# Softmax sums of batches 2 to 7: VectorE copies and additions in place of four TensorE products per batch

## The chip, the cores and the metric

The kernel runs on one core of a Trainium2 chip. The metric is the device time of one execution in microseconds (us). TensorE is called PE in the profile (its weight loads PEld), VectorE is DVE, ScalarE is ACT, GpSimd is POOL, and SyncE, which only issues DMAs here, is SP.

## The reference

Grouped-query attention (8 batches, 16 query heads on 4 key heads, 384 positions, head size 64) feeds a mixture of experts with a gate in two levels (4 groups of 4 experts; 3072 tokens of width 1024).

```python
scores = scale * np.matmul(q, k.transpose(0, 1, 3, 2))      # k, v repeated for each group of heads
scores = scores - np.max(scores, axis=-1, keepdims=True)
attn = np.exp(scores)
attn = attn / (np.sum(attn, axis=-1, keepdims=True) + 1e-09)
x = np.matmul(attn, v)                                       # then (B, S, H*D) -> (3072, 1024)

g_idx = np.argmax(x @ w_group, axis=1)                       # per token: a group, then an expert in it
for g in range(G):
    xg = x[g_idx == g]
    e_idx = np.argmax(xg @ w_expert[g], axis=1)
    for e in range(Eg):
        h = np.maximum(xg[e_idx == e] @ w1[g, e], 0.0)
        ye = h @ w2[g, e]
        out[tokens of (g, e)] = (g_w * e_w)[:, None] * ye    # softmax weights of the picks
```

## The kernel before

The order of the work on every engine is written out by hand. The batches are staggered: while the attention of batch b ends, the expert products of batch b-1 run.

**Attention.** A batch has 24 steps (NU). In a step PE makes score products (`score`, L310) into a PSUM tile of the ring "s", ScalarE takes their exponential into a tile `e` (L316), and PE multiplies that with V (`pv`, L329) into a tile of the ring "o". Each ring has two PSUM tiles, taken in turn by `ps_tile`, so the next but one user of a ring waits until a tile's reader is done. `e` is not divided by its sum: that is done on the product.

**Sums of the softmax.** GpSimd adds the `e` tiles of two steps (`pair`, L337), VectorE reduces each result to 24 numbers per partition (`reduce`, L346, into `red3`), and `join_keys` (L399) adds the three parts into `red` of 128 partitions x 96. On a partition of `red` lies a partial sum of one of two query heads r (partitions 64r to 64r+63), and each quarter of 32 partitions holds half of the keys. So two quarters have yet to be added, and the result is wanted on four quarters: `normalise` transposes blocks of 32x32 of its reciprocal, `inv`, spread over a row (L423), and multiplies x with it (L427). `sums` (L404 to L416) does both with PE: two fp32 products with the constant matrix `half32`, which the trace shows as four, into a tile of "o", and two reciprocals from PSUM into `inv`.

**The block between two attentions** (`block`, L808) sets the order around the change. PE gets, in order: expert products of batch b-1 (`moe_h`, L604: four groups of 16 products, each into an "s" tile, with ScalarE's relu behind it), the sum products of batch b behind the second group, the third and fourth group, the second expert matrix for three blocks of tokens (`ffn_y`, L618), the gate products of batch b (`gate_logits`, L442, which read all of x), the first two score products of batch b+1, and the third block of tokens. VectorE gets the join, the sums, four transposes and four multiplications (`normalise`), and then the gate's softmax, some 20 small instructions. ScalarE gets four relus, the four casts of x to bf16 (`cast`, L432, each behind one `normalise`), and between and after them the scaling of two output tiles (`y_out`, L637), then the exponentials of the first scores. The first output tile's scaling stands between the second and third cast, the second's behind the last cast. The rings run on here: the two score products take the two "s" tiles that `y_out` reads.

Batch 2 differs: in its block VectorE does the whole gate softmax of batch 1 (`gate_softmax`, `out_weights`) between the join and the sums.

GpSimd issues the fetches of the next weights, K and Q in the block (L514, L520, L96, L101), and between them sums V (`sum_v`, L112 to L114). Batches 0 and 1 have orders of their own and call `sums` too; so does a loop at the end for tokens whose expert was not fetched.

Of the kernel before, what the change touches and what calls it, by code (L numbers as in the profile page):

```python
# [9 lines left out]
F32 = mybir.dt.float32  # L10
# [8 lines left out]
def kernel(  # L19
# [11 lines left out]
    nc = tc.nc  # L31
    P = 128
    B, Hq, S, D = q.shape
    _, Hkv, _, _ = k.shape
# [5 lines left out]
    KQ = DM // P  # L40
# [7 lines left out]
    NB = S // 32  # L48
# [11 lines left out]
    gpool = ctx.enter_context(tc.tile_pool(name="gate", bufs=1))  # L60
# [7 lines left out]
    def ps_tile(which, shape=None, dtype=F32):  # L68
        if which == "x":
            which = f"o{1 - turn['o']}"  # L70
        else:
            turn[which] = 1 - turn[which]
            which += str(turn[which])
        return psum.tile(shape or [P, 2, 512], dtype, name="ps_" + which)
# [5 lines left out]
    def rows(x):  # L80
        return x.rearrange("h (p c) d -> (h p) (c d)", c=NC).rearrange("(a p) n -> p a n", p=P)
# [13 lines left out]
    def load_k(b, src=None):  # L95
        nc.gpsimd.dma_start(out=k_pad[:, D:(NK + 1) * D].rearrange("p (a n) -> p a n", n=NC * D),  # L96
                            in_=rows(k[b] if src is None else src))

    def load_q(b, src=None):
        qraw[b] = lpool.tile([P, KQ, NC * D], BF16, name="q_raw")  # L100
        nc.gpsimd.dma_start(out=qraw[b], in_=rows(q[b] if src is None else src))  # L101

    def load_v(b, src=None):
        vraw[b] = vpool.tile([P, NA, NC * D], F32, name="v_raw")
        nc.sync.dma_start(out=vraw[b], in_=rows(v[b] if src is None else src))

    def sum_v(b):
        t = gpool.tile([P, NA * D], BF16, name="vsum")
        s = gpool.tile([P, NA, NC // 2 * D], F32, name="vs")
        v_ = vraw[b]  # L110
        hn = NC // 2 * D
        nc.gpsimd.tensor_add(out=s, in0=v_[:, :, :hn], in1=v_[:, :, hn:])  # L112
        nc.gpsimd.tensor_add(out=s[:, :, :D], in0=s[:, :, :D], in1=s[:, :, D:2 * D])
        nc.gpsimd.tensor_add(out=t.rearrange("p (h d) -> p h d", d=D), in0=s[:, :, :D],  # L114
                             in1=s[:, :, 2 * D:])
        vsum[b] = t
# [59 lines left out]
    for g in range(2, Hkv):  # L176
        nc.gpsimd.dma_start(out=qraw[0][:, KG * g:KG * (g + 1)],
                            in_=rows(q[0])[:, KG * g:KG * (g + 1)])
# [113 lines left out]
    xT, xb, red3, parts = {}, {}, {}, {}  # L292
# [99 lines left out]
    red, inv = {}, {}  # L392

    def join_keys(b, g0, g1):
        if b not in red:
            red[b] = gpool.tile([P, Hkv, 2, NB], F32, name="red", bufs=2)
        same = len(set(parts[b][g0:g1])) == 1
        for g, h in [(g0, g1)] if same else [(g, g + 1) for g in range(g0, g1)]:
            nc.vector.tensor_reduce(  # L399
                out=red[b][:, g:h].rearrange("p g t j -> p g (t j)"),  # L400
                in_=red3[b][:, g:h, :parts[b][g]].rearrange("p g c t j -> p g (t j) c"),
                axis=AX.X, op=ALU.add)

    def sums(b, g0, g1, which):  # L404
        sm = ps_tile(which)[:, :, :(g1 - g0) * 2 * NB]
        for r in range(2):
            nc.tensor.matmul(out=sm[:, r], lhsT=half32[:, r, :],  # L407
                             rhs=red[b][:, g0:g1].rearrange("p g t j -> p (g t j)"),
                             start=True, stop=True)
        if b not in inv:  # L410
            inv[b] = gpool.tile([P, KQ, NB], F32, name="inv", bufs=2)
        iv = inv[b][:, 2 * g0:2 * g1].rearrange("p (g r) j -> p r g j", r=2)
        sm = sm.rearrange("p r (g t j) -> p r g t j", t=2, j=NB)
        for t in range(2):
            ts = slice(t * D, (t + 1) * D)
            nc.vector.reciprocal(out=iv[ts], in_=sm[ts, :, :, t])  # L416

    def normalise(b, m, which=None, eng=nc.vector):
        if b not in xb:
            xb[b] = xpool.tile([P, KQ, S], BF16, name="xb")  # L420
        ks = slice(2 * m, 2 * m + 2)
        rb = ps_tile(which)[:, :, :S] if which else epool.tile([P, 2, S], F32, name="e")
        nc.vector.transpose(  # L423
            out=rb.rearrange("p k (j x) -> p k j x", x=32),
            in_=inv[b][:, ks].unsqueeze(3).to_broadcast([P, 2, NB, 32]))
        x = xT[b][:, ks, :]
        eng.tensor_mul(out=x, in0=x, in1=rb)  # L427

    def cast(b, m, eng=None):
        ks = slice(2 * m, 2 * m + 2)  # L430
        if eng is None:
            nc.scalar.copy(out=xb[b][:, ks, :], in_=xT[b][:, ks, :])  # L432
        else:
            eng.tensor_copy(out=xb[b][:, ks, :], in_=xT[b][:, ks, :])
# [11 lines left out]
    def guess_mean(b, pt):  # L446
        pm = pt[:, 1, :2]
        nc.tensor.matmul(out=pm, lhsT=vsum[b], rhs=halfb, start=True, stop=True)
        vm = gpool.tile([P, 2], BF16, name="vm")
        nc.vector.tensor_copy(out=vm, in_=pm)  # L450
        return vm
# [6 lines left out]
    def guess_out(pt):  # L458
        return pt[:, 1, 64:64 + NW]
# [110 lines left out]
    def after_transposes(b):  # L570
        t = gpool.tile([1, 1], BF16, name="tok")
        nc.gpsimd.tensor_copy(out=t, in_=qT[b][0:1, KQ * SC - 1, P - 1:P])

    def pick_w1(b):
        w1s[b] = fetch1(ers[b])

    def pick_w2(b):
        w2s[b] = fetch2(ers[b])

    def out_weights(b):  # L580
        m = gpool.tile([P, SC, NE], F32, name="m")
        nc.vector.tensor_tensor(out=m, in0=cw_all[:, b],
                                in1=oh1_all[:, b, :].unsqueeze(1).to_broadcast([P, SC, NE]),
                                op=ALU.mult)
        we = gpool.tile([P, SC], F32, name="we", bufs=2)
        nc.vector.tensor_reduce(out=we, in_=m, axis=AX.X, op=ALU.add)
        weff[b] = we
# [25 lines left out]
    def ffn_y(w2, hT, c, which, nhs=(0, 1), y=None):  # L613
        if y is None:
            y = ps_tile(which)
        for nh in nhs:
            for f in range(FQ):
                nc.tensor.matmul(out=y[:, nh, :], lhsT=hT[:, f, c * P:(c + 1) * P],  # L618
                                 rhs=w2[:, f, nh * HALF:(nh + 1) * HALF],
                                 start=(f == 0), stop=(f == FQ - 1))  # L620
        return y
# [3 lines left out]
    def moe_h(b, f0, which):  # L625
        if f0 == 0:
            hTs[b] = xpool.tile([P, FQ, S], BF16, name="hT", bufs=1)
        ffn_h(xb[b], w1s[b], hTs[b], f0, which)
# [12 lines left out]
    def moe_y(b, c, which):  # L641
        y_out(b, c, ffn_y(w2s[b], hTs[b], c, which))

    def do(f, *a):
        return lambda: f(*a)
# [162 lines left out]
    def block(b):  # L808
        last = b == B - 1
        f = b - 1  # L810
        if b + 2 < B:
            load_v(b + 2)
        if not last:
            after_transposes(b + 1)
        pick_w1(b)
        pick_w2(b)
        if not last:
            sum_v(b + 1)
        if b + 2 < B:
            load_k(b + 2)  # L820
            load_q(b + 2)
        moe_h(f, 0, "s")
        at[b].reduce(NU - 1)
        join_keys(b, 0, Hkv)
        if b == 2:
            gate_softmax(1, state["gl"], False)()
            out_weights(1)
        moe_h(f, 2, "s")
        sums(b, 0, Hkv, "o")
        normalise(b, 0)  # L830
        normalise(b, 1)
        moe_h(f, 4, "s")
        normalise(b, 2)
        moe_h(f, 6, "s")
        cast(b, 0)
        cast(b, 1)
        normalise(b, 3)
        moe_y(f, 0, "s")
        cast(b, 2)
        pt = ps_tile("o")  # L840
        y = ffn_y(w2s[f], hTs[f], 1, "s", (0,))
        vm = None if last else guess_mean(b + 1, pt)
        ffn_y(w2s[f], hTs[f], 1, "s", (1,), y)
        cast(b, 3)
        y_out(f, 1, y)
        gate_logits(b, pt)
        if not last:
            guess_logits(vm, guess_out(pt))
            at[b + 1] = Attn(b + 1)
            at[b + 1].score(0)  # L850
            at[b + 1].score(1)
        w = gate_softmax(b, gate_rows(pt, not last), not last)
        if not last:
            pick(b + 1)
            pick_index(b + 1)
            read_pick(b + 1)
        w()
        out_weights(b)
        y = ffn_y(w2s[f], hTs[f], 2, "o")
        if last:  # L860
            y_out(f, 2, y)
            return {}
        return {1: [do(y_out, f, 2, y, True)]}
# [51 lines left out]
    with tc.If(n_left > 0):  # L915
        with tc.For_i(0, n_left, 1):
# [38 lines left out]
            for m_ in range(Hkv):  # L955
# [6 lines left out]
                                    in1=oh.unsqueeze(2).to_broadcast([P, B, SC, NE]), op=ALU.mult)  # L962
# [49 lines left out]
```

## Time and profile before

| | |
|---|---|
| three runs | 363.31, 365.40, 365.44 us (median 365.4) |
| the profiled execution | 363.79 us |
| its span, first to last instruction | 361.2 us |
| PE busy | 352.7 us (98%) |
| VectorE busy | 244.3 us (68%) |
| ScalarE busy | 224.6 us (62%) |
| GpSimd busy | 222.8 us (62%) |
| granted TensorE clock, mean | 0.997 of full speed |

Times in the trace are microseconds from the span's start. A busy share is an average over the whole span; which engine matters in a stretch is read from that stretch.

### The profile page before, as it was taken

The page shows a single profiled execution, that of the slowest core. Times are in us where ns is not written, and L with a number is a line of the kernel's source. Part 1 is how long each engine was busy: PE and PEld are TensorE (multiplying, and loading weights), DVE is VectorE, ACT ScalarE, POOL GpSimd, SP SyncE. Part 2 cuts the span into 40 slices and gives each one's busy share as a digit, 9 for nine tenths or more (in the row PEclk, how much of TensorE's full clock was granted, in tenths as well). Part 3 has the DMA queues.
Part 4 walks back from the last instruction along what each step waited for, and adds up shares of the span by engine and source line. Part 5 has one row for each costly group of instructions (what it writes and reads, how often), then busy time and mean ns, then how long its engine had stood idle before and what let it go on. Part 6 is the DMA issues. An engine that isn't in the chain of part 4 may idle for free.

```text
span 361.2 us, 9178 instructions
## 1 busy us (share of the span) xinstructions
PE 352.7 (98%) x3823; PEld 185.0 (51%) x3823; DVE 244.3 (68%) x462; ACT 224.6 (62%) x296; POOL 222.8 (62%) x175
## 2 busy tenths in 40 slices
PE   7999999999999999999999999999999999999994
PEld 3445555445454545654555455555546545555542
DVE  5487678785788676847679477775668577784031
ACT  4799855389725695367934599265972669534321
POOL 8889975959937399705993089911996049910000
PEclk9999999999999999999999999999999999999998
DMA  8998999699999999999999999899996992099925
GB/s 201 183 155 148 228 195 146 127 242 238 208 188 159 248 211 172 210 208 255 195 198 198 226 232 168 180 210 243 207 183 100 200 260 86 2 162 213 265 56 125
DMA packets 69485, 67.14 MB, mean 186 GB/s; under 512 B 37144, under 2 KB 49688, under 8 KB 69440
## 3 DMA queue, kind: packets, MB, share of 16 engines
q0 software_dynamic: 26640, 41.03, 65.6%
q1 hardware_dynamic: 42288, 24.88, 30.9%
q8 instruction: 32, 0.52, 0.5%
q10 hardware_dynamic: 512, 0.61, 0.5%
q14 instruction: 13, 0.11, 0.1%
HBM read 86.07 MB, written 12.58 MB: 273 GB/s over the span
## 4 chain that ended last, share of the span: by engine, by line
PE 90%; ACT 3%; DVE 3%; POOL 1%; issue 1%; POOLq 0%; ACTq 0%
PE ps_o L329 31%; PE ps_s L604 20%; PE ps_s L618 13%; PE ps_s L310 9%; PE ps_o L618 6%; PE ps_o L442 3%; ACT e L316 2%; PE ps_s L892 2%; PE ps_o L604 1%; PE ps_o L407 1%; PE ps_o L892 1%; PE ps_o L270 1%; POOL e L337 1%; DVE ps_o L423 1%; DVE red L346 1%
## 5 line engine op out<-in xcount | busy, mean ns | idle before, releaser
L337 POOL TENSOR_TENSOR e<-e 128x768 f32<-128x768 f32 x91 | 162.7, 1826 | 76.4 <-PE ps_s L310 70.4
L316 ACT ACTIVATE e<-ps_s 128x768 f32<-128x768 f32 x187 | 147.6, 813 | 22.4 <-PE ps_s L310 20.3
L329 PE MATMUL ps_o<-e,v_raw 64*64 64x384 f32 x1496 | 149.1, 482 | 0.1
L346 DVE TRANSPOSE_TENSOR_REDUCE red<-e 128x24 f32<-128x768 f32 x95 | 91.8, 973 | 39.8 <-POOL e L337 39.6
L604 PE MATMUL ps_s<-xb,w 128*128 128x384 bf16 x480 | 80.9, 326 | 0.1
L329 PEld LDWEIGHTS ps_o<-e,v_raw 64*64 64x64 f32 x1496 | 54.3, 133 | 37.2 <-issue 29.5
L604 PEld LDWEIGHTS <-w 128*128 128x128 bf16 x512 | 49.4, 98 | 35.7 <-issue 4.5
L310 PE MATMUL ps_s<-qT,kT 64*64 64x384 bf16 x768 | 64.1, 327 | 1.0 <-ACT e L316 0.7
L618 PEld LDWEIGHTS <-hT 128*128 128x128 bf16 x336 | 31.8, 98 | 38.9 <-issue 2.4
L608 ACT ACTIVATE hT<-ps_s 128x768 bf16<-128x768 f32 x23 | 18.6, 810 | 52.7 <-PE ps_s L604 49.3
L618 PE MATMUL ps_s<-w,hT 128*128 128x512 bf16 x224 | 49.8, 379 | 0.0
L310 PEld LDWEIGHTS <-kT 64*64 64x64 bf16 x768 | 23.8, 105 | 36.2 <-issue 34.0
L618 PE MATMUL ps_o<-w,hT 128*128 128x512 bf16 x112 | 25.6, 380 | 0.0
L637 ACT ACTIVATE ot<-ps_s,we 128x1024 f32<-128x1024 f32 x14 | 15.6, 1115 | 15.7 <-PE ps_s L618 15.7
L423 DVE STREAM_TRANSPOSE e<-inv 128x768 f32<-128x768 f32 x26 | 25.2, 971 | 0.2
L371 DVE COPY xT<-ps_o 128x768 f32<-128x768 f32 x26 | 24.0, 924 | 1.6 <-PE ps_o L329 1.3
L432 ACT CAST xb<-xT 128x768 bf16<-128x768 f32 x28 | 22.3, 833 | 2.8 <-DVE xT L427 2.8
L427 DVE TENSOR_TENSOR xT<-xT,e 128x768 f32<-128x768 f32 x24 | 23.2, 969 | 0.8
L416 DVE RECIPROCAL inv<-ps_o 64x96 f32<-64x96 f32 (+2 forms) x20 | 12.7, 635 | 8.4 <-PE ps_o L407 8.2
L463 DVE STREAM_TRANSPOSE gl<-ps_o 128x96 f32<-128x96 f32 x8 | 2.3, 283 | 20.9 <-PE ps_o L455 16.3
L611 ACT ACTIVATE hT<-ps_s 128x384 bf16<-128x384 f32 x14 | 6.1, 488 | 12.5 <-PE ps_s L604 12.5
L442 PEld LDWEIGHTS ps_o<-xT,wg 128*32 128x32 f32 x448 | 9.2, 110 | 3.1 <-issue 2.7
(133 smaller groups left out, 222.8 us busy)
## 6 DMA issues: line engine op xcount, KB each, us to landing
w<-in_moe_w_dram POOLq DMA_DIRECT2D x16, 2048.0 KB, 21.8
out_dram<-ot SPq DMA_DIRECT2D x42, 256.0 KB, 7.0
q_raw<-in_q_dram POOLq DMA_DIRECT2D x7, 768.0 KB, 28.1
v_raw<-in_v_dram SPq DMA_DIRECT2D x7, 384.0 KB, 5.5
k_raw<-in_k_dram POOLq DMA_DIRECT2D x7, 192.0 KB, 24.3
out_dram<-ot SPq DMA_DIRECT2D x10, 128.0 KB, 2.4
w<-in_q_dram POOLq DMA_DIRECT2D x3, 192.0 KB, 6.3
w<-in_k_dram SPq DMA_DIRECT2D x2, 192.0 KB, 3.6
```

What stands on the lines that cost most here:

```text
L310: nc.tensor.matmul(out=sT[r * H2:(r + 1) * H2, s, :S], lhsT=kT[b][s * D:(s + 1) * D, key_block(b, s, g // 2, c), ks], rhs=qT[b][s * D:(s + ...
L316: nc.scalar.activation(e.rearrange("p t (s x) -> p s t x", s=2), sT[:, :, :S].rearrange("p s (t x) -> p s t x", t=2), ACT.Exp, scale=scale)
L329: nc.tensor.matmul(out=oT[t * D:(t + 1) * D, r, :S], lhsT=vraw[b][r * H2:(r + 1) * H2, g // 2, c * D:(c + 1) * D], rhs=self.e[u][r * H2:(r ...
L337: nc.gpsimd.tensor_add(out=self.e[u - 1], in0=self.e[u - 1], in1=self.e[u])
L346: nc.vector.tensor_reduce(out=red3[b][:, g, parts[b][g]].rearrange("p t j -> p (t j)"), in_=self.e[w].rearrange("p t (j x) -> p (t j) x", ...
L371: nc.vector.tensor_copy(out=dst, in_=src)
L423: nc.vector.transpose(out=rb.rearrange("p k (j x) -> p k j x", x=32), in_=inv[b][:, ks].unsqueeze(3).to_broadcast([P, 2, NB, 32]))
L427: eng.tensor_mul(out=x, in0=x, in1=rb)
L432: nc.scalar.copy(out=xb[b][:, ks, :], in_=xT[b][:, ks, :])
L442: nc.tensor.matmul(out=pt[32 * t:32 * t + 32, 0, :S // 4], lhsT=wg[:, head_pair(m), :], rhs=x[:, t], start=(m == 0), stop=(m == KQ - 1))
L604: nc.tensor.matmul(out=h[:, jj, :S], lhsT=w1[:, head_pair(m), (f0 + jj) * P:(f0 + jj + 1) * P], rhs=x[:, m, :], start=(m == 0), stop=(m == ...
L618: nc.tensor.matmul(out=y[:, nh, :], lhsT=hT[:, f, c * P:(c + 1) * P], rhs=w2[:, f, nh * HALF:(nh + 1) * HALF], start=(f == 0), stop=(f == ...
```

## The change

In `block`, that is for batches 2 to 7, `sums` gives way to a new function, which does the same on VectorE alone. For each r it copies the quarter with the second half of the keys onto the partitions of the first, into PSUM, and adds the two, with the result in a slot of `red3` that these batches don't use. One reciprocal over 64 partitions follows, and eight copies of 32x48 spread the result over the four quarters of `inv`. A tile of "o" is still taken, now written and read by VectorE. Its place in the order of the calls is the same.

```diff
+    Q = P // 4
+
+    def sums_copied(b, which):
+        r_, sm = red[b], red3[b][:2 * Q, :, 4]
+        sw = ps_tile(which)[:, 0, :Hkv * 2 * NB].rearrange("p (g t j) -> p g t j", t=2, j=NB)
+        for r in range(2):
+            lo, hi = slice(2 * r * Q, (2 * r + 1) * Q), slice((2 * r + 1) * Q, (2 * r + 2) * Q)
+            nc.vector.tensor_copy(out=sw[lo], in_=r_[hi])
+            nc.vector.tensor_add(out=sm[r * Q:(r + 1) * Q], in0=r_[lo], in1=sw[lo])
+        nc.vector.reciprocal(out=sm, in_=sm)
+        inv[b] = gpool.tile([P, KQ, NB], F32, name="inv", bufs=2)
+        for r in range(2):
+            for h in range(4):
+                nc.vector.tensor_copy(out=inv[b][h * Q:(h + 1) * Q, r::2, :],
+                                      in_=sm[r * Q:(r + 1) * Q, :, h // 2, :])
...
         moe_h(f, 2, "s")
-        sums(b, 0, Hkv, "o")
+        sums_copied(b, "o")
         normalise(b, 0)
```

## Rows read from the trace of the kernel before

**Rows 1.** Window (us, busy PE, PEld, DVE, ACT, POOL; clock, DMA); the page's chain.
```profile
184.50:227.00 42.50, 42.50 (x472) 22.22 (x471) 29.82 (x54) 27.72 (x36) 26.75 (x21) 1.00 1.10 206
...
PE 90%; ACT 3%; DVE 3%; POOL 1%; issue 1%; POOLq 0%; ACTq 0%
```

**Rows 2.** Timeline of PE, batch 4: start, duration, then line and what.
```profile
184.27 5.37 PE L604 MATMUL ps_s<-xb,w 128*128 128x384 bf16 x32
189.48 0.58 PE L407 MATMUL ps_o<-red,half 128*128 128x96 f32 x4
189.90 5.36 PE L604 MATMUL ps_s<-xb,w 128*128 128x384 bf16 x32
195.10 5.34 PE L618 MATMUL ps_s<-w,hT 128*128 128x512 bf16 x24
...
203.72 0.52 PE L310 MATMUL ps_s<-qT,kT 64*64 64x384 bf16 x8
```

**Rows 3.** Timeline of PE, batch 2.
```profile
98.64 5.37 PE L604 MATMUL ps_s<-xb,w 128*128 128x384 bf16 x32
104.61 5.36 PE L604 MATMUL ps_s<-xb,w 128*128 128x384 bf16 x32
...
118.44 0.52 PE L310 MATMUL ps_s<-qT,kT 64*64 64x384 bf16 x8
```

**Rows 4.** Groups by line, VectorE: busy us, mean ns of one, idle before.
```profile
L416 DVE RECIPROCAL inv<-ps_o 64x96 f32<-64x96 f32 x14 | 10.6, 754 | 6.2 <-PE ps_o L407 6.1
L634 DVE TENSOR_SCALAR ot<-ps_o,we 128x512 f32<-128x512 f32 x10 | 7.0, 742 | 0.0
L218 DVE COPY half<-half 64x96 f32<-64x96 f32 x2 | 0.5, 247 | 0.1
L236 DVE TENSOR_TENSOR wgs<-wg,ps_o 128x80 f32<-128x80 f32 x1 | 0.2, 236 | 0.0
L211 DVE COPY mod<-mod 128x64 f32<-128x64 f32 x1 | 0.2, 196 | 0.0
```

**Rows 5.** Timeline of VectorE, batch 4.
```profile
188.74 0.48 DVE L399 TENSOR_REDUCE red<-red 128x96 f32<-128x288 f32 x1
190.10 1.52 DVE L416 RECIPROCAL inv<-ps_o 64x96 f32<-64x96 f32 x2 [0.88 <-PE ps_o L407]
191.66 0.98 DVE L423 STREAM_TRANSPOSE e<-inv 128x768 f32<-128x768 f32 x1
...
198.32 0.96 DVE L427 TENSOR_TENSOR xT<-xT,e 128x768 f32<-128x768 f32 x1
...
208.46 1.40 DVE L634 TENSOR_SCALAR ot<-ps_o,we 128x512 f32<-128x512 f32 x2
```

**Rows 6.** Timeline of VectorE, batch 2.
```profile
107.03 1.51 DVE L416 RECIPROCAL inv<-ps_o 64x96 f32<-64x96 f32 x2
108.57 0.98 DVE L423 STREAM_TRANSPOSE e<-inv 128x768 f32<-128x768 f32 x1
...
115.44 0.96 DVE L427 TENSOR_TENSOR xT<-xT,e 128x768 f32<-128x768 f32 x1
```

**Rows 7.** Timeline of VectorE and GpSimd, 7 to 9 us.
```profile
7.59 0.99 POOL L112 TENSOR_TENSOR vs<-v_raw 128x384 f32<-128x384 f32 x1 [0.75 <-DMA v_raw<-in_v_dram]
...
7.62 1.01 DVE L216 TENSOR_TENSOR half<-mod 64x32 f32<-64x32 f32 x1
```

**Rows 8.** Timeline of GpSimd, batches 2 and 4.
```profile
110.07 1.54 POOL L112 TENSOR_TENSOR vs<-v_raw 128x384 f32<-128x384 f32 x1
...
190.74 0.45 POOL L113 TENSOR_TENSOR vs<-vs 128x128 f32<-128x128 f32 x1
```

**Rows 9.** Timeline of ScalarE, batch 2.
```profile
116.43 0.83 ACT L432 CAST xb<-xT 128x768 bf16<-128x768 f32 x1 [1.05 <-DVE xT L427]
117.17 1.11 ACT L637 ACTIVATE ot<-ps_s,we 128x1024 f32<-128x1024 f32 x1
```

**Rows 10.** Timeline of ScalarE, batch 4.
```profile
202.23 1.11 ACT L637 ACTIVATE ot<-ps_s,we 128x1024 f32<-128x1024 f32 x1 [0.91 <-PE ps_s L618]
```

## The prediction, before the kernel was run

> **What bounds the kernel now.** I read the windows of one period of the steady batches first. In the stretch that holds batch 4's block, PE is busy for all of its 42.50 us, VectorE for 29.82 and GpSimd for 26.75, and the chain that ended last lies on PE for 90% of the span [rows 1]. What shortens PE's stream there is worth its full length, and VectorE's time costs nothing until something on PE's path waits for it. So the change takes work from the engine that sets the end and gives more to one with room; the question is where VectorE's room runs out. For that I read the timelines of PE, VectorE and ScalarE side by side in batch 4, which stands for 3 to 7, and again in batch 2, whose block is different.
>
> **What is removed.** In batch 4 the first two expert groups (32 products each) start at 184.27 and 189.90, and the second pair's successor at 195.10 [rows 2]. 32 products alone take 195.10 - 189.90 = 5.20 us; the first 32 with the four sum products behind them take 5.63. The four cost 0.43 us of PE. In batch 2 the same distance is 104.61 - 98.64 = 5.97 [rows 3]: 0.77 us, because PE also stood waiting for the joined sums there. So -0.43 us for each of batches 3 to 7, and -0.77 for batch 2, if nothing else is late: 5 x 0.43 + 0.77 = 2.92 us. Batches 0 and 1 keep their products. Two reciprocals of 64x96 (0.754 us each, [rows 4]) leave VectorE too, with the wait for PE ahead of them.
>
> **What is added.** VectorE now runs thirteen instructions in a row: two copies of 32x96 into PSUM, two additions of 32x96, one reciprocal of 64x96, eight copies of 32x48. I call T the time from the start of the first to the start of the transpose that follows. From [rows 4]: a copy of 96 elements is 0.247 us (the 64x96 row); an addition of 80 with one PSUM operand is 0.236, so some 0.26 for 96; a reciprocal of 64x96 is 0.754; a copy of 64 elements is 0.196, and by the slope to the 96 row one of 48 is 0.17. Sum: 2 x 0.247 + 2 x 0.26 + 0.754 + 8 x 0.17 = 3.13 us. Steps between instructions come on top. The two old reciprocals write different halves of the partitions and do not overlap: two of 0.754 fill 1.52, and the next starts about 0.03 later [rows 4, 5, 6]. Two instructions of y_out, both on all partitions, do overlap: 2 x 0.742 take 1.40 [rows 4, 5]. The new copies change their starting partition each time, so I take the first row: 13 x 0.03 = 0.4, T = 3.5 us. The other end is the overlap of 0.08 at each of seven steps between copies: T = 2.9. The Trainium skill, VectorE: DVE Perf Modes, section Two Vector instructions with no wait between them, says that an instruction which starts in another group of 32 partitions than the last one of its memory is held until all before it are done; by that rule T is the 3.5 and not the 2.9, and these two pairs agree with it.
>
> **GpSimd beside it.** The copies from SBUF to SBUF may have to share with GpSimd. At 7.62 an addition of 64x32, which should take under 0.24 us, took 1.01 beside a GpSimd addition that had started at 7.59 and took 0.99 [rows 4, 7]: VectorE waited about 0.8. In batch 4 the eight copies would begin at about 191.2, where GpSimd runs the sums of V (L113 from 190.74, the next behind it); in batch 2 they would run from 109.0 to 110.5, and L112 starts at 110.07 and took 1.54 instead of 0.99, beside a VectorE multiplication [rows 7, 8]. Whether small copies are hit is not shown. The ends are nothing and +1.5 (L112 and L113 both waited for); I take 0.5, which is nearer to nothing, because the copies are short and most start before L112 does: T = 4.0. The Trainium skill, SBUF — State Buffer, section Who interferes with whom, has copies in their two-port mode and GpSimd exclude each other for a whole instruction, whoever is first; by that rule alone T would be some 4.5 in batch 2, which would lose 0.5 us more, and rival (b) below is that rule met several times over. The 1.01 us row agrees with it for an addition; no row has a copy in that place.
>
> **Where VectorE's delay lands, batches 3 to 7.** In batch 4 the joined sums end at 188.74 + 0.48, so the new run can start at 189.26; the transpose starts at 191.66 now [rows 5]. The old stage takes 2.40, and the delay is T - 2.40 = 1.6 us. The last multiplication then ends at 199.28 + 1.6 = 200.9 [rows 5]. Who needs it? ScalarE's last cast (0.74 long, [rows 9]), and behind it in ScalarE's queue the scaling of the y tile, which starts at 202.23 and would start 0.43 earlier with PE [rows 10]: 199.28 + 0.03 + 0.74 = 200.05 against 201.80 leaves 1.75 us. If that is late, the second score product of the next batch is next: it writes the PSUM tile that the scaling reads. It starts half of the eight score products (0.52 us) after their first, at 203.72 + 0.26, and the scaling ends at 203.34 [rows 2, 10], which is 0.59 more with 0.05 for the hand-over. The gate products, which stand right ahead of the first score product, need the last quarter of x only for their own last quarter, shortly before 203.72 [rows 2]: over 2 us after 200.9. PE feels nothing below a delay of 2.34, T = 4.74. So these batches give 0.43 each, 2.15 us together; batch 7 has no scores behind it and still more room.
>
> **Batch 2 is the expensive one.** Here VectorE does the whole gate softmax of batch 1 between the join and the sums, so its reciprocals start at 107.03, long after PE's products, and no wait for PE is saved: the old stage is 108.57 - 107.03 = 1.54 us [rows 6], the delay T - 1.54 = 2.5. And there is no cover: the last cast already waits 1.05 us for VectorE's last multiplication (ends 115.44 + 0.96 = 116.40) and starts at 116.43, the y scaling follows at once at 117.17 and ends at 118.28 [rows 6, 9], and the second score product starts at about 118.44 + 0.26 = 118.70 [rows 3]. That is 0.42 of room, 0.37 after the hand-over. The cast, the scaling and the second score product all move with VectorE, and PE, in order, stands before that product. Batch 2 does not gain 0.77; it loses T - 1.54 - 0.37 = 4.0 - 1.91 = 2.1 us.
>
> **The sum.** -2.15 + 2.1 = about 0. The profiled execution took 363.8 us for its span of 361.2; the three runs have a median of 365.4, the lowest 363.3. I predict 365.3. By T: 2.9 gives -2.15 + 1.0 = -1.2 (364.2); 5.0 gives batch 2 +3.1, batches 3 to 6 -0.17 each and batch 7 -0.43, together +2.0 (367.4). Runs of one kernel differ by 2 us, so nothing within 1% (3.65 us) can be told from no change.
>
> **Rivals.**
> (a) The thirteen instructions are much cheaper than their nearest rows, T about 2.2, with the copies sliding over each other. Then batch 2 loses 0.3 and the whole gains 1.9: 363.5. Against it: the reciprocal and the four instructions ahead of it depend on one another and take 1.8 us alone, which leaves 0.05 for each copy, and the smallest copy of [rows 4] takes 0.196. Chance 0.12.
> (b) Slower. GpSimd's fetches and additions break into the run of copies in every batch, so that T passes 4.74 and batches 3 to 6 lose as well: each -0.43 + (T - 4.74). All of it is then 4 x (T - 5.17) - 0.43 + T - 1.91, which reaches +3.65 at T = 5.33; at T = 6 it is 7.0 us, 372. For it: the 1.01 us addition, and GpSimd has work at that place in batches 2 to 6. Against it: it takes two or more GpSimd instructions waited for in full, in each batch. Chance 0.07.
> (c) The change does not free PE: something else was due where the products stood. Each third expert group refills the first group's PSUM tile, and starts as soon as ScalarE has emptied it. If such a wait took the 0.43 us, batches 3 to 7 give nothing and batch 2 still loses 2.1: 367.5. Against it: the group's first 32 products end at 189.5 and follow without a gap today. Chance 0.04.
>
> **How the numbers follow.** The forecast (T from 2.9 to 5.0) has 0.77. Its own ends are 364.2 and 367.4; the lower end of the range goes on to rival (a) and to the spread of the runs, 362.9. Faster by over 1% needs more than the whole 2.92: 0.04, a measurement's accident; slower by over 1% is (b) with a little of (c): 0.08; the rest, 0.88, is within 1%.
>
> **What would show it.** PE: no sum products behind batch 2's first two expert groups, and 5.20 us between their starts. VectorE: thirteen small instructions, 3.5 to 4 us to the transpose, copies of about 0.17, longer where GpSimd is busy. Batches 3 to 6: periods 0.43 us shorter and no new wait of PE. Batch 2: PE idle before the second score product, with ScalarE's scaling as what ended it, and that product about 2 us later than 118.70. Wrong would be: copies of 0.1 us or of 0.5; PE waiting in batch 4; or no wait in batch 2, which would mean that the casts are not what holds the score.

## The result and the profile after

The changed kernel takes 368.31 us (median of 7 runs, 366.56 to 368.73) against 365.06 for the kernel before (7 runs, 363.25 to 365.44). The ratio is 1.011, with a 95% interval of 1.0083 to 1.0138. It is slower, by a little over 1%, and lies above the range of the prediction. The profiled execution took 366.63 us for a span of 364.8, where before it was 363.79 for 361.2; the time grew by 2.8 us and the span by 3.6. The lines of the changed functions moved: the joined sums are L425 to L431, the transpose L439, the multiplication L443, the last cast L448, the gate products L458, the expert products L620 and L634, the scaling L653.

The first thing to read is where the 3.6 us of span came in. The start of the gate products is a good mark for that, because each batch has one; both timelines of PE give:

| stretch | before, us | after, us | difference |
|---|---|---|---|
| span's start to batch 1's gate products | 82.49 | 82.31 | -0.18 |
| batch 1's to batch 2's | 34.35 | 37.78 | +3.43 |
| batch 2's to batch 3's | 42.64 | 43.75 | +1.11 |
| batch 3's to batch 7's, four distances | 170.55 | 168.88 | -1.67 |
| batch 7's to the end of PE's last product | 26.08 | 26.08 | 0.00 |
| from there to the span's end | 5.1 | 6.0 | +0.9 |

So the steady batches gain 0.42 each. Batch 2 loses more than they bring, a second loss of 1.5 us stands right behind it (1.11 and the 0.42 that this distance should have gained), and the tail, from PE's last product to the end of the span, is longer. PE's last product ends 2.7 us later (356.11 and 358.80), which is nearly all of the 2.8 by which the time grew. Most of the tail's 0.9 does not count in the time: outside the span lie 363.79 - 361.2 = 2.6 us before and 366.63 - 364.8 = 1.8 after.

The timeline of PE in the changed kernel, batch 2 and then batch 4:

```profile
98.45 10.57 PE L620 MATMUL ps_s<-xb,w 128*128 128x384 bf16 x64
108.86 5.34 PE L634 MATMUL ps_s<-w,hT 128*128 128x512 bf16 x24
...
114.07 1.89 PE L634 MATMUL ps_s<-w,hT 128*128 128x512 bf16 x8
120.09 1.84 PE L458 MATMUL ps_o<-xT,wg 128*32 128x96 f32 x64 [4.14 <-DVE vm L466]
...
122.03 0.85 PE L310 MATMUL ps_s<-qT,kT 64*64 64x384 bf16 x8
122.81 4.48 PE L634 MATMUL ps_o<-w,hT 128*128 128x512 bf16 x16
...
188.63 10.57 PE L620 MATMUL ps_s<-xb,w 128*128 128x384 bf16 x64
199.04 5.34 PE L634 MATMUL ps_s<-w,hT 128*128 128x512 bf16 x24
...
206.06 1.53 PE L458 MATMUL ps_o<-xT,wg 128*32 128x96 f32 x64
```

The sum products are gone: 64 expert products stand in one row, and in batch 4 the next group starts 10.41 us after their first, where it was 195.10 - 184.27 = 10.83 [rows 2]. In batch 2 PE then stands for 4.14 us, and it stands ahead of the gate products, not behind them. The gate products and all that follows are also longer than in batch 4 (1.84 against 1.53). The windows from the wait on show why. In each row the granted clock stands behind the busy times of the five engines, the third number from the end:

```profile
119.00:120.00 1.00, 0.00 (x0) 0.00 (x0) 0.97 (x2) 0.12 (x1) 0.00 (x0) 1.00 1.11 207
...
121.00:122.00 1.00, 1.00 (x34) 0.72 (x22) 0.00 (x0) 0.73 (x1) 0.00 (x0) 0.58 1.06 180
122.00:123.00 1.00, 1.00 (x11) 0.32 (x10) 0.76 (x5) 0.33 (x1) 0.00 (x0) 0.50 0.99 137
123.00:124.00 1.00, 1.00 (x3) 0.30 (x2) 0.86 (x5) 1.00 (x2) 0.00 (x0) 0.50 1.09 291
124.00:125.00 1.00, 1.00 (x5) 0.42 (x4) 0.83 (x6) 0.38 (x2) 0.00 (x0) 0.72 1.08 293
125.00:126.00 1.00, 1.00 (x6) 0.46 (x5) 0.86 (x7) 0.00 (x0) 0.00 (x0) 1.00 1.07 287
```

After the wait the clock was granted at half (1.2 GHz instead of 2.4) for some 3.4 us (the shares 0.58 and 0.72 give 121.2 to 124.6), in which PE is busy throughout and does half as much. That is the 1.5 us behind batch 2.

VectorE in batch 2, batch 4 and batch 7, which answers to [rows 5] and [rows 6]:

```profile
106.93 0.25 DVE L425 COPY ps_o<-red 32x96 f32<-32x96 f32 x1
107.21 0.24 DVE L426 TENSOR_TENSOR red<-red,ps_o 32x96 f32<-32x96 f32 x1
...
108.07 0.75 DVE L427 RECIPROCAL red<-red 64x96 f32<-64x96 f32 x1
108.85 3.35 DVE L431 COPY inv<-red 32x48 f32<-32x48 f32 x8
112.23 0.98 DVE L439 STREAM_TRANSPOSE e<-inv 128x768 f32<-128x768 f32 x1
...
118.89 0.96 DVE L443 TENSOR_TENSOR xT<-xT,e 128x768 f32<-128x768 f32 x1
119.88 0.16 DVE L466 CAST vm<-ps_o 128x2 bf16<-128x2 f32 x1
...
193.60 0.25 DVE L425 COPY ps_o<-red 32x96 f32<-32x96 f32 x1
...
195.52 2.19 DVE L431 COPY inv<-red 32x48 f32<-32x48 f32 x8
197.75 0.98 DVE L439 STREAM_TRANSPOSE e<-inv 128x768 f32<-128x768 f32 x1
...
205.39 0.16 DVE L466 CAST vm<-ps_o 128x2 bf16<-128x2 f32 x1
...
320.28 0.25 DVE L425 COPY ps_o<-red 32x96 f32<-32x96 f32 x1
...
322.20 1.52 DVE L431 COPY inv<-red 32x48 f32<-32x48 f32 x8
323.75 0.98 DVE L439 STREAM_TRANSPOSE e<-inv 128x768 f32<-128x768 f32 x1
```

T is 323.75 - 320.28 = 3.47 us in batch 7, 197.75 - 193.60 = 4.15 in batch 4 and 112.23 - 106.93 = 5.30 in batch 2. All of the difference is in the eight copies: 1.52, 2.19 and 3.35 us. What differs is GpSimd beside them, here in batch 2 (it has nothing in batch 7's place):

```profile
108.75 0.88 POOL L536 DMA_DIRECT2D w<-in_moe_w_dram  x1
109.65 1.01 POOL L112 TENSOR_TENSOR vs<-v_raw 128x384 f32<-128x384 f32 x1
110.74 0.48 POOL L113 TENSOR_TENSOR vs<-vs 128x128 f32<-128x128 f32 x1
111.30 0.47 POOL L114 TENSOR_TENSOR vsum<-vs 128x128 bf16<-128x128 f32 x1
```

The copies run from the fetch to the last of three additions. One by one, four of the eight take 0.18 us, as all do in batch 7; the others take 0.79, 1.05, 0.35 and 0.35, and each of these ends within 0.06 us behind the end of the fetch or of one of the additions. Their excess, 0.61 + 0.87 + 0.17 + 0.17, is the 1.8 us by which T is longer. In batches 3 to 5 the copies meet one addition and the fetches of K and Q instead. The chain that ended last has taken VectorE in (before it was 90% PE and 3% VectorE [rows 1]):

```profile
PE 84%; DVE 7%; ACT 3%; POOL 1%; issue 1%; DMA 1%; ACTq 0%; POOLq 0%
```

### The profile page after: what moved, and what is told of

It reads as the page before. It is cut to its first block, busy times and chain, and to the rows that moved or that the text cites. A ratio compares the mean times of both kernels' runs of the same rounds, so it can differ in the third digit from the quotient of the medians.

```text
span 364.8 us, 9196 instructions
## 1 busy us (share of the span) xinstructions
PE 351.0 (96%) x3799; PEld 182.0 (50%) x3799; DVE 257.6 (71%) x528; ACT 225.5 (62%) x296; POOL 220.8 (61%) x175
## 4 chain that ended last, share of the span: by engine, by line
PE 84%; DVE 7%; ACT 3%; POOL 1%; issue 1%; DMA 1%; ACTq 0%; POOLq 0%
PE ps_o L329 30%; PE ps_s L620 18%; PE ps_s L634 11%; PE ps_s L310 9%; PE ps_o L634 6%; PE ps_o L458 3%; ACT e L316 2%; PE ps_s L908 2%; PE ps_o L620 1%; DVE xT L443 1%; PE ps_o L908 1%; DMA w<-in_q_dram 1%; DVE e L439 1%; POOL e L337 1%; DVE inv L431 1%
## 5 line engine op out<-in xcount | busy, mean ns | idle before, releaser
L620 PE MATMUL ps_s<-xb,w 128*128 128x384 bf16 x480 | 79.9, 326 | 0.1
L620 PEld LDWEIGHTS <-w 128*128 128x128 bf16 x512 | 49.4, 98 | 36.5 <-issue 4.5
L634 PEld LDWEIGHTS <-hT 128*128 128x128 bf16 x336 | 32.1, 98 | 39.8 <-issue 3.8
L634 PE MATMUL ps_s<-w,hT 128*128 128x512 bf16 x224 | 49.8, 379 | 0.0
L448 ACT CAST xb<-xT 128x768 bf16<-128x768 f32 x28 | 23.3, 831 | 13.1 <-DVE xT L443 13.0
L634 PE MATMUL ps_o<-w,hT 128*128 128x512 bf16 x112 | 26.4, 389 | 0.0
L439 DVE STREAM_TRANSPOSE e<-inv 128x768 f32<-128x768 f32 x26 | 25.2, 972 | 0.2
L443 DVE TENSOR_TENSOR xT<-xT,e 128x768 f32<-128x768 f32 x24 | 23.0, 958 | 0.8
L653 ACT ACTIVATE ot<-ps_s,we 128x1024 f32<-128x1024 f32 x14 | 15.6, 1114 | 8.9 <-PE ps_s L634 8.9
L458 PE MATMUL ps_o<-xT,wg 128*32 128x96 f32 x448 | 11.0, 251 | 4.1 <-DVE vm L466 4.1
L431 DVE COPY inv<-red 32x48 f32<-32x48 f32 x48 | 12.5, 261 | 0.8
```

The costliest lines, as they stand in the source:

```text
L439: nc.vector.transpose(out=rb.rearrange("p k (j x) -> p k j x", x=32), in_=inv[b][:, ks].unsqueeze(3).to_broadcast([P, 2, NB, 32]))
L458: nc.tensor.matmul(out=pt[32 * t:32 * t + 32, 0, :S // 4], lhsT=wg[:, head_pair(m), :], rhs=x[:, t], start=(m == 0), stop=(m == KQ - 1))
L620: nc.tensor.matmul(out=h[:, jj, :S], lhsT=w1[:, head_pair(m), (f0 + jj) * P:(f0 + jj + 1) * P], rhs=x[:, m, :], start=(m == 0), stop=(m == ...
```

## The experiments

The theory after this result: (1) the removed products give what was forecast; (2) eight copies from SBUF to SBUF are held by each GpSimd instruction that they meet; (3) in batch 2 the gate products stand behind VectorE's cast to `vm`, not the score product behind ScalarE; (4) PE's long wait halves the clock, which costs again. The rivals: the loss is spread over all batches, by copies that are dear everywhere; the wait is ScalarE's, as forecast; the clock is an accident of one execution.

**Which batches lose.** Two kernels split the change: one keeps the products in batch 2 (below), the other, with b > 2 in the condition, changes batch 2 alone.

```diff
-        sums_copied(b, "o")
+        if b == 2:
+            sums(b, 0, Hkv, "o")
+        else:
+            sums_copied(b, "o")
```

> Batch 2 keeps the sum products on PE, batches 3 to 7 have the copies. Theory 1 (the loss is all in batch 2, and the other batches gain what their products took): five times 0.42 us less than before, about 363 us, 0.994 of before, and no long wait of PE at batch 2's gate products. Rival (every batch loses a little, by longer copies or by what they do to GpSimd): at or above before, 365 to 368 us.

> Only batch 2 has the copies, batches 3 to 7 keep the products. Theory 1: batch 2's loss without the gains of the others, so 2.1 us above the changed kernel: about 370.4 us, 1.015 of before, with a PE wait of about 4 us ahead of batch 2's gate products and a granted clock at half behind it. Rival (every batch loses a little): one sixth of the change's +3.3 to +4.0, so about 365.7 us.

With batch 2's products kept: 363.06 us, ratio 0.998 (0.9958 to 1.0002). With batch 2 alone changed: 369.89 us, ratio 1.0178 (1.0139 to 1.0216). So batch 2 makes the whole loss; that the first kernel is faster than the one before is not shown by its times, whose interval reaches 1. In the first kernel the four distances between gate products from batch 3 on are 42.20 to 42.23 us; the distance to batch 3 is 42.89, because that batch's copies now met the fetch and the three additions (3.33 us for the eight, T = 5.28) and PE waited there, in the same place as in batch 2:

```profile
159.55 1.53 PE L458 MATMUL ps_o<-xT,wg 128*32 128x96 f32 x64 [0.60 <-DVE vm L466]
```

Nothing slows down behind this wait. In the second kernel the wait is 3.96 us, the clock is at half from 118.9 to 125.7, at first while PE still stood, and the next distance is 45.19 instead of 42.65: 2.5 us. The clock costs more there than in the changed kernel's profile, so its price is not fixed.

**The copies against GpSimd.** The reciprocal is written into the PSUM tile that is there already, and the eight copies read from it.

```diff
-        nc.vector.reciprocal(out=sm, in_=sm)
+        sp = sw[:2 * Q]
+        nc.vector.reciprocal(out=sp, in_=sm)
...
-                                      in_=sm[r * Q:(r + 1) * Q, :, h // 2, :])
+                                      in_=sp[r * Q:(r + 1) * Q, :, h // 2, :])
```

> As the changed kernel, but the reciprocal is written to the PSUM tile and the eight copies read it there, so that no copy has SBUF on both sides. Theory 1 (the copies are held up by GpSimd's instructions on SBUF): each copy takes about 0.19 us in every batch, as in batch 7 where GpSimd is idle, T is about 3.5 us in batches 2 to 7 alike instead of 5.3 in batch 2 and 4.15 in 3 to 5; PE's wait in batch 2 falls from 4.1 to about 2.3 us, the clock stays at full, and the whole takes about 364.5 us. Rival (copies of 32x48 from SBUF, with changing partitions, are slow of themselves, or the delay in batch 2 has another cause): T stays above 4 us in batch 2 and the time near 368 us.

364.9 us, ratio 1.0033 (1.0011 to 1.0056) to the kernel before. The groups by line and form, first the changed kernel and then this one, give the busy time and the mean of one copy, over all six batches:

```profile
L431 DVE COPY inv<-red 32x48 f32<-32x48 f32 x48 | 12.5, 261 | 0.8
```

```profile
L432 DVE COPY inv<-ps_o 32x48 f32<-32x48 f32 x48 | 9.6, 200 | 0.8
```

In batch 2 the eight take 1.69 us, beside two fetches and the first addition, and T is 3.64; in the five other blocks they take 1.69 to the last digit, whatever GpSimd does. The copies' excess was GpSimd's doing. It is still PE's wait for `vm`, now 2.49 us, that follows, and the clock falls to half all the same (timeline of PE and the windows, this kernel):

```profile
118.33 2.79 PE L459 MATMUL ps_o<-xT,wg 128*32 128x96 f32 x64 [2.49 <-DVE vm L467]
...
119.00:120.00 1.00, 1.00 (x36) 1.00 (x30) 0.00 (x0) 0.96 (x1) 0.00 (x0) 0.50 1.21 190
120.00:121.00 1.00, 1.00 (x28) 0.77 (x20) 0.00 (x0) 0.00 (x0) 0.00 (x0) 0.50 0.96 145
```

The gate products take 2.79 instead of 1.53, and the next distance is 43.75 where the following ones are 42.23: 1.5 us again. The mean granted clocks of its 12 runs hint that this is not so in every execution: the one at 0.998 took 362.58 us, those at 0.990 took 365.84 and 366.04. The mean takes in the end of the span too, where the clock is at half in every profile, so it does not give the price.

**What the gate products wait for.** The cast to `vm` reads the second bank of the PSUM tile into which the gate products write the first. In this kernel it is put before VectorE's last transpose and multiplication, and the product that it reads before the block of products that stood ahead of it.

```diff
-        normalise(b, 3)
         moe_y(f, 0, "s")
-        cast(b, 2)
         pt = ps_tile("o")
-        y = ffn_y(w2s[f], hTs[f], 1, "s", (0,))
         vm = None if last else guess_mean(b + 1, pt)
+        normalise(b, 3)
+        cast(b, 2)
+        y = ffn_y(w2s[f], hTs[f], 1, "s", (0,))
```

> As the changed kernel, but the product and the VectorE cast of the guessed mean (into the same PSUM tile as the gate products) are issued ahead of the last normalisation, not behind it. Theory 1 (the gate products wait as a whole for that cast, because it reads their PSUM tile): in batch 2 PE's wait ends about 1.9 us earlier, near 118.2, and splits, the rest of it ahead of the last quarter of the gate products; the end moves by 0.6 us, or by about 2 where the clock then stays at full: 366.3 to 367.7 us. Rival (the gate products wait for the last multiplication of x as a whole): one wait of about 4 us as before, 368.3 us.

368.32 us, ratio 1.011 (1.0074 to 1.0146): no gain. But the timelines of VectorE and PE show the dependence:

```profile
118.49 0.16 DVE L466 CAST vm<-ps_o 128x2 bf16<-128x2 f32 x1
...
119.57 0.96 DVE L443 TENSOR_TENSOR xT<-xT,e 128x768 f32<-128x768 f32 x1
...
118.71 2.75 PE L458 MATMUL ps_o<-xT,wg 128*32 128x96 f32 x64 [2.69 <-DVE vm L466]
...
122.46 0.53 PE L310 MATMUL ps_s<-qT,kT 64*64 64x384 bf16 x4 [0.39 <-ACT ot L653]
```

The gate products start 0.06 us after the cast has ended and 1.8 us before the last multiplication ends (120.53), so it is the cast that holds them. Behind it the forecast wait comes out: the second half of the score products waits for ScalarE's scaling. Only, the wait ahead of the gate is still 2.69 us (the eight copies took 3.77 here), and the clock was at half from 119.1 to 125.9, longer than in the changed kernel; the next distance is 45.85.

**Both together.** Copies from PSUM and the earlier cast.

> The changed kernel with the copies from PSUM and the guessed mean's cast ahead of the last normalisation, the gate softmax in its old place. Theory 1: the gate products of batch 2 start after 0.4 us of waiting, wait again for some 0.9 ahead of their last quarter, and the second score product waits some 1.2 for ScalarE's scaling of the y tile, which is what the prediction held to be the only wait. No wait is above 1.3 us, so the clock stays at full, unlike with the single wait of 2.5 us: batch 2 loses 1.5 us, the others gain 2.1, together 0.998 of before, about 363 us. Rival (the clock falls for the sum of the waits, not for one long one): about 364.9, as with the copies from PSUM alone.

363.73 us, ratio 1.0006 (0.9982 to 1.0029). The timeline of PE:

```profile
116.64 1.20 PE L459 MATMUL ps_o<-xT,wg 128*32 128x96 f32 x48 [0.61 <-DVE vm L467]
118.52 0.54 PE L459 MATMUL ps_o<-xT,wg 128*32 128x96 f32 x16 [0.68 <-DVE xT L444]
...
120.39 0.36 PE L310 MATMUL ps_s<-qT,kT 64*64 64x384 bf16 x4 [0.91 <-ACT ot L654]
```

This is the order of waits that the prediction had: the gate's last quarter waits for its own part of x, and the score for ScalarE. They sum to 2.20 us, not much less than the single 2.49 of the kernel with PSUM copies alone, but every window from 115 to 122 shows a granted clock of 1.00, and the products keep their length. That it matters how the waiting is cut up is read from this pair of profiles alone.

**A way round batch 2's block.** VectorE's gate softmax of batch 1 stands between the join and the sums. Three kernels move it into the attention of batch 2, two steps of which issue it: the kernel before with that move, the changed kernel with it, and the changed kernel with PSUM copies and it. A fourth, with PSUM copies, moves only the nine VectorE instructions that stand ahead of ScalarE's part, to one earlier step.

```diff
+    def second_softmax():
+        state["w"] = gate_softmax(1, state["gl"], False)
+
+    def second_weights():
+        state["w"]()
+        out_weights(1)
...
+        10: [second_softmax],
+        14: [second_weights],
...
-        if b == 2:
-            gate_softmax(1, state["gl"], False)()
-            out_weights(1)
```

> The kernel before, with nothing but the gate softmax of batch 1 (VectorE instructions, its exponential on ScalarE and the output weights) moved from batch 2's block into steps 10 and 14 of batch 2's attention, where VectorE waits for GpSimd every second step. Batch 2 then looks like the others: its sum products cost 0.43 us instead of 0.77 and its VectorE chain ends some 3 us earlier. Theory 1 (nothing but VectorE's order made batch 2 tight): -0.3 us, 0.999 of before. Rival (the small instructions hold up the reductions and the scores): slower by 1 us or more.

> The changed kernel with the same move. Theory 1 (the loss of the change is VectorE's late start in batch 2): the sums start at about 103.9 instead of 106.9, no wait of PE at batch 2's gate products, clock at full; batch 2 gains 0.77 and the others 0.42 each, less some 0.6 in batch 3 where GpSimd holds up the copies: 2.2 us less than before, 0.994, about 361.3 us, 7 us less than the changed kernel. Rival (the copies lose wherever they stand in batch 2): near the changed kernel's 368 us.

> As the run before it, with the copies reading PSUM. Theory 1: all of the 2.9 us that the products cost in six batches, no wait of PE at any gate product: 0.992 of before, about 360.6 us. If the tail behind PE's last product (5.1 us before, 6 us and more in the changed kernels) belongs to the change and not to the run, 1 us less of it: 0.995.

The times were 368.9 us (ratio 1.0153, 1.0117 to 1.0189), 366.58 (1.0087, 1.0053 to 1.0121) and 366.37 (1.0077, 1.0048 to 1.0106). The move costs by itself, in the kernel before as well. The small instructions of VectorE now meet GpSimd's additions of `e`, which follow each other without a gap (five in 8.90 us); the timeline of VectorE in the kernel before with the move, and PE's wait that comes of it:

```profile
89.56 1.74 DVE L479 TENSOR_SCALAR ohg<-sh 128x12 f32<-128x12 f32 x1
91.33 1.77 DVE L481 TENSOR_TENSOR pr<-gl,ohg 128x48 f32<-128x48 f32 x1
93.14 0.23 DVE L484 TENSOR_REDUCE el<-pr 128x12 f32<-128x48 f32 x1
...
95.83 0.36 PE L310 MATMUL ps_s<-qT,kT 64*64 64x384 bf16 x4 [3.01 <-ACT e L316]
```

In the block the first two take 0.17 and 0.21 us. ScalarE, which does the exponential of this softmax in order with the others, waited 3.38 us for it, and PE waited for ScalarE; the clock was at half from 96.8 to 100.2. But the pair tells what the joined sums do without batch 2's handicap: from batch 1's gate products to batch 7's it is 252.24 us with products and 249.35 with copies, -2.89 us. That this is near the prediction's first sum of -2.92 is luck in part. From batch 2's gate on it is 5 x 0.42 = 2.1, and batch 2's block gains 0.43 like the others (its expert groups start 5.63 us apart with products, 5.20 without), together 2.5; the other 0.4 stands ahead of the block, in the attention, where the waits that the move makes fall differently. With PSUM copies the same distance is 249.88, -2.36. None of the three waits at a gate.

> The copies from PSUM in all six batches; of batch 1's gate softmax only the nine VectorE instructions ahead of the exponential are moved, to step 7 of batch 2's attention, and the exponential and what follows stay in the block. Theory 1: ScalarE never waits for VectorE in the attention, so PE does not either; VectorE starts the sums of batch 2 some 1.9 us earlier, the gate products of batch 2 wait under 0.6 us and the clock stays at full: 2 to 2.5 us less than before, 0.994, less if the tail is longer. Rival: the moved instructions are held up by GpSimd's additions as long as in the two runs before (up to 1.8 us each), VectorE's reductions run late to the end of the attention and the sums start no earlier: near 365 us.

The fourth took 369.67 us, ratio 1.0163 (1.0116 to 1.0209). Leaving ScalarE's part in the block did not help: four of the nine VectorE instructions took 1.73 to 1.78 us each, VectorE's copy of the attention's result out of PSUM came late, and PE waited for that:

```profile
99.69 1.56 PE L329 MATMUL ps_o<-e,v_raw 64*64 64x384 f32 x8 [5.53 <-DVE xT L371]
```

**The version for this kernel.** Products in batch 2, copies from PSUM in batches 3 to 7; and the kernel before once more, for its tail.

> Batch 2 keeps the products on PE, batches 3 to 7 have the copies, read from PSUM. Against the run with batch 2's products and copies from SBUF it should lose the 0.6 us wait of batch 3. Theory 1: five times 0.42 us less up to PE's last gate products, all gate distances 42.2 us but batch 2's; with a tail behind PE like that of the kernel before, 0.994 of before (361.4 us); with 1 us more of tail, 0.997 (362.4 us). Rival (the copies from PSUM cost elsewhere): no better than 0.998.

> The kernel before, unchanged, for a second look at the tail between PE's last product and the span's end. If the tail belongs to the run, it differs from the first look's 5.1 us by up to 1 us; if it belongs to the change, it is 5.1 us again.

362.78 us, ratio 0.9968 (0.9946 to 0.9991): faster than both kernels, against the kernel before by 363.54 - 362.78 = 0.76 us of the medians or 0.3% by the ratio. No wait of PE is new, and each distance from batch 2's gate on is 42.2 us (timeline of PE, batch 3):

```profile
158.87 1.53 PE L459 MATMUL ps_o<-xT,wg 128*32 128x96 f32 x64
```

That is 2.1 us less up to batch 7's gate products; 1.9 of it are given back between PE's last product and the end of the span, 7.0 us here, and 0.8 of that comes back outside the span (362.58 - 360.8 = 1.8 us against 2.6 before). The kernel before, run once more, took 363.14 us (span 361.0) with a tail of 5.1.

## Why the prediction was wrong

The forecast was a change of about 0; PE's last product came 2.7 us later. Two terms of its sum failed: GpSimd's share of T in batch 2, put at 0.5 us and measured at 1.8, and the clock behind PE's wait, put at nothing without a word and measured at 1.5. A third step, what PE waits for in batch 2, was wrong as well; it moved the size by 0.2 us only, but it gathered the waiting into one piece ahead of the gate.

- **Removed work: right.** -0.43 for each of batches 3 to 7 was forecast, 0.42 measured. For batch 2 -0.77 was forecast and 0.7 is seen: its 4.14 us of waiting shows as 3.43, and 3.96 as 3.26 in the kernel with batch 2 alone.
- **T without GpSimd: right.** 3.5 was forecast and 3.47 measured. The two ways of counting the steps were 3.5 and 2.9 (which is 3.5 less the overlaps; with the overlaps in place of the steps between the copies it is about 2.7); the copies, which change their starting partition each time, take the longer. The Trainium skill, VectorE: DVE Perf Modes, section Two Vector instructions with no wait between them, which holds such an instruction until all before it are done, agrees with this 3.47.
- **GpSimd beside the copies: mis-sized.** The step "the ends are nothing and +1.5; I take 0.5 ... because the copies are short and most start before L112 does" failed. In batches 3 to 5 it was 0.7, in batch 2 it was 5.30 - 3.5 = 1.8, beyond the upper end, since the copies met the fetch at 108.75 and all three additions. L112 and L113, which made up that end, were waited for and cost 1.04; the fetch with 0.61 and L114 with 0.17 were not counted. With the sources in PSUM the same place took 3.64. This is 1.3 us of the loss. The Trainium skill, SBUF — State Buffer, section Who interferes with whom, says that a copy in a two-port mode and GpSimd shut each other out for a whole instruction and that an instruction with at most one SBUF input outside those modes does not contend; 3.35 us from SBUF against 1.69 from PSUM agrees. The prediction named that rule, and gave it too small a share.
- **Where batch 2's delay lands: the place was wrong, its size nearly right.** "The gate products ... need the last quarter of x only for their own last quarter" overlooked that VectorE's cast to `vm` stands behind the last multiplication and reads the tile that the gate products write; the whole of them waits for it. Neither the list of the block's work ahead of the prediction nor its rows have this cast. The score product that the prediction had in view is held 0.2 us less by its own chain (0.03 + 0.74 + 1.11 + 0.05 = 1.93 us through ScalarE, against 0.03 + 0.16 + 0.05, then 161.15 - 159.55 = 1.60 to the first score product and 0.26 to the second, 2.1). So the forecast loss, T - 1.91, gives 3.4 with the T of 5.30, and 3.43 was measured; that it fits through the wrong chain is luck, since the two chains differ by only 0.2 us. By the kernels with the earlier cast the chain through ScalarE is there and comes second.
- **What a single wait does to the clock: not thought of.** The prediction took PE's wait as the whole price. In the profile 1.53 us follow at half the clock, in the kernel with batch 2 alone 2.5. Joined with `vm`'s place this matters: one wait of 2.49 us brought the clock down, three of 0.61, 0.68 and 0.91 us in a row did not.
- **The room in batches 3 to 6: held.** It was put at T = 4.74. In batch 4, T was 4.15 and the cast to `vm` ended 206.06 - 205.55 = 0.5 us before the gate products, so the bound is about 4.65, by another chain than forecast. In the kernel with batch 2's products, batch 3 had 5.28 and waited 0.60 us, near 5.28 - 4.65 = 0.63.
- **The tail: not thought of,** +0.9 us of the span, of which about 0.8 is missing again outside it in this pair of executions; its cause is open.

The sum, by the forecast's terms: about 0, plus 1.3 for GpSimd, 1.5 for the clock and 0.9 for the tail, less 0.18 at the start, is 3.5 us; the span grew by 3.6. In the time, which grew by 2.8, the tail is worth 0.15. The range ended at 367.4, and GpSimd alone would have brought the forecast of 365.3 to 366.6, inside it; with the clock it is 368.1, beside the measured median of 368.31. That median lies 1.7 us above the profiled execution, as that of the kernel before lies 1.3 above its own. The runs' mean granted clocks go from 0.986 to 0.993, the slowest (368.73) having the lowest, so the clock's price may vary between runs; that was not traced. Rival (b) had the right mechanism, and the wrong scope and size: it needed every batch to be broken into, where only batch 2 went past its room, and GpSimd's part was less than half of the loss.

## What to carry to other kernels

Before work is moved to an engine with room, look for the one stage that has none (a different order at the start of a pipeline, here batch 2), and list everything that stands behind the delayed instruction in that engine's queue, the smallest too: whoever writes the PSUM tile that a two-column cast reads waits for it, as here PE did. On VectorE, the small SBUF copies beside GpSimd were priced by the GpSimd instructions that they met and not by their size: eight took 1.52 us alone and 3.2 to 3.8 in batch 2. Read from PSUM they took 1.69 wherever they stood. Where a wait of a few microseconds on PE cannot be avoided, several short ones may be cheaper than one (one pair of profiles says so), and the clock's row behind it belongs to the price.

## What the hardware showed that was not expected

- In all eight profiles in which PE stood once for 2.49 to 5.53 us, a granted clock of half followed the wait or joined its second half, for 3.4 to 6.8 us (2.49: from 118.3 to 121.8; 2.69: 119.1 to 125.9; 3.01: 96.8 to 100.2; 3.96: 118.9 to 125.7; 4.14: 121.2 to 124.6; 5.53: 97.6 to 104.4). In the five others it stayed at 1.00 up to PE's last product. The stretch does not grow with the wait in these runs. Two of these five have waits, one of 0.60 us and three of 0.61, 0.68 and 0.91 in a row. What lies between was not tried.
- VectorE instructions of 0.17 to 0.21 us took 1.73 to 1.78 between back-to-back GpSimd additions, each held for about one addition (five in 8.90 us), while a reduction in the same place took 0.23.
- The stretch from PE's last product to the end of the span is 4.9 to 5.1 us in the three profiles with products in all batches and 5.9 to 7.2 in all ten with copies in any, though the instructions there are the same. One of the two last stores of 32 KB takes longer to land: the slower of them 2.2 to 2.3 us in the three, 3.1 to 3.8 in the ten. In return less time lies outside the span, by the medians of the runs 2.2 us in the kernels with products in all batches and 1.8 in eight of the ten others (1.9 and 2.1 in two), so about 0.4 of the longer tail is not in the times. Here the slower store, in the changed kernel and then in the kernel before run once more (line, engine, count, size, median us from issue to landing). Why is open; no run tells it apart.

```profile
out_dram<-ot ACTq DMA_DIRECT2D x1, 32.0 KB, 3.3
```

```profile
out_dram<-ot ACTq DMA_DIRECT2D x1, 32.0 KB, 2.3
```
